# A written-out instruction order for attention plus a gated MLP on one core: no-ops between the halves of matmul pairs allowed on four queues, and a new order

## The chip, the core and the metric

The kernel runs on one core of a Trainium2 chip. The metric is the device time of one execution in microseconds. Three runs of the kernel before gave 153.65, 155.31 and 155.96 us; their median, 155.31 us, is the time before.

The core has five instruction queues that matter here: TensorE (PE in the profile), VectorE (DVE), ScalarE (ACT), GpSimd (POOL) and SyncE (SP). Each works through its own instructions strictly in order, and they wait for each other through semaphores. SP does no arithmetic; it issues transfers. POOL also issues transfers.

## What is computed

One row of 2048 tokens, 448 wide, bf16 inputs. Cut to what matters:

```python
xn = layernorm(x)                                    # (2048, 448)
q, k, v = split(xn @ wqkv)                           # 16 heads of 28
# each token attends to 8 keys: itself and 2, 4, .. 14 tokens back
attn = softmax(einsum(q, k[gathered]) * 28 ** -0.5)  # masked where the index is negative
s = (attn @ v[gathered]) @ wo                        # (2048, 448)
g = silu(gelu(xn @ w1 + b1) @ w2 + b2)               # 448 -> 1792 -> 448
return x + s * g
```

## The kernel before: tiles, stages and what sets the order

Tokens are kept even ones first, odd ones second, so that a dilated window of 8 becomes a contiguous one. They are cut into 16 row tiles of 128 tokens, four to a chunk of 512; the chunks are numbered 0 to 3. The attention works instead in nine blocks of up to 228 queries, each with two halves (p = 0 and 1).

For every row tile t: the statistics of its rows (L353, L357) and the reciprocal deviation (L374 and L375 on POOL, four tiles at a time from tile 8 on) give the normalised rows `xn` (L387). For tiles 0 to 3 TensorE transposes them (L402); from tile 4 on a transposing transfer issued by SP does (L300, `xnT<-xn`). The buffer of `xn` has four slots, so a fifth tile is normalised only when the transfer of an earlier one has landed. From `xnT` come the projections: q and k (L478), v (L501), and the first layer of the MLP (L551, 14 column tiles m of 128 per chunk). Projected q and k are copied from PSUM to row-major tiles by ACT (L249) or DVE (L251), and one transposing transfer per row tile on SP (L300, `qkT<-qk_tok` or `qk_pair`) brings them into `qkT`. Projected v goes to DRAM by POOL (L294, `v_rows<-v_tok`) and comes back shifted, per block (L294, `v<-v_rows`).

A block of attention is: copies of its keys (L662), scores (L677), exponentials on ACT (L683), a mask multiply on DVE or POOL (L693), the sum over values (L708), a reciprocal and a scaling on DVE (L719, L724), a store of the rows to DRAM (L731, by POOL or SP), and a transposing read of two row tiles at a time (L300, `xnT<-o_rows` or `oT<-o_rows`). The second layer of the MLP (L577, and L603 for the last four tiles) needs both halves of `w2`, that is both 784 KB transfers of L287 (tasks S260 and S262); its bias is added on DVE (L619). The output projection (L742, L757) and the gating (L765, L767, L773) end a tile.

**Pairs.** Inner dimensions such as 448 = 3 * 128 + 64 leave half of the 128 rows of TensorE empty, so most matmuls are run as pairs `pair(a, b)` (L425) of two jobs, each using 64 rows. The first half of a pair (f1, task P) runs job a on the upper rows and job b on the lower rows, into two PSUM banks; the second half (f3, task P) swaps them, and it accumulates into the same banks. Between the halves stands a no-op on another queue (f2, L437): it waits for the last matmuls of the first half, and the second half waits for it.

```python
def f2(k):
    held["told"] = (nc.gpsimd if k.on == "POOL" else nc.sync).nop()
    for i in held["last"]:
        behind(held["told"], i)
```

The no-op costs its queue nothing but its place: whatever stands ahead of it on that queue comes first, and whatever stands behind it waits until the first half has ended.

**Order.** All work is 1032 tasks, numbered as they are added (`_Plan.add`, L85). `ORDER` (L17 to L62) lists every task once, as a letter for the engine and the number: P TensorE, V DVE, A ACT, G POOL, S SP, D the landing of a transfer (no instruction). `emit` (L98) goes through it and issues the instructions, so the position of a task in its engine's queue, the PSUM banks and buffer slots that it takes (first freed, first used) and, where a task allows several engines, the engine are all set by that text. The text is fixed; the kernel holds no planner and no cost model.

Before, 49 of the 61 no-ops are on POOL and 12 on SP: chunks 0 and 1 allow POOL alone, the rest either (`HOPS`, L14).

The tasks that the text below names:

| task | what it is |
| --- | --- |
| S258, S256 | loads of x for row tiles 12 to 15 and 8 to 11, 448 KB each |
| S262, S260 | loads of the two halves of w2, 784 KB each |
| S161, S207, S214, S230, S237, S425 | transposing transfers of q and k of row tiles 3, 4, 5, 6, 7, 13 |
| S333, S337 | transposing transfers of xn of row tiles 10 and 11 |
| S929 | transposing read of attention rows of row tiles 4 and 5 |
| V229 / A229, P472 | copy of k of row tile 6 out of PSUM; first half of MLP layer 1, chunk 1, m = 0 and 1, which reuses its bank |
| P502, no-op 503, P504 | the pair of MLP layer 1, chunk 1, m = 12 and 13 |
| P209, no-op 210, P211 | the pair q, k of row tile 5 |
| P362, no-op 363, P364 | the pair q, k of row tile 10 |
| P436, no-op 437, P438 | the pair q, k of row tile 14 |
| P577 | first half of MLP layer 2 for row tiles 0 and 1 |
| V740, V589, P701 | first key copy of block 3; bias of row tile 2 of layer 2; value sum of block 1, p = 1 |
| P782 | value sum of block 4, p = 0 |
| G431, G460, G804, P812 | v of row tile 12 to DRAM; v of block 6 from DRAM; a mask of block 5; value sum of block 5, p = 0 |
| G278 | reciprocal deviation of row tiles 8 to 11 |

Of the kernel before, what the change touches and what calls it, by code (L numbers as in the profile page):

```python
# [18 lines left out]
G98 P5 S40 D41 S44 D45 P6 S46 D47 P7 G100 P8 V58 P9 V59 S74 D75 V62 A60 P10 S76 D77 P11 V61 V102 P12 P13 G649 V103 P14  # L19
V63 P104 A64 P105 G27 V106 A107 D108 S78 D79 G28 V65 P128 G31 V109 G29 V110 G30 P111 P112 V113 S80 D81 P132 A114 D115  # L20
P129 S84 D85 V66 P184 P133 V67 V70 A68 S86 D87 P130 V69 V116 P131 V117 V71 V185 P118 V101 A72 P119 V99 A52 V120 D121
S88 D89 P134 V73 V122 P149 V123 V136 A135 V146 P124 G150 P125 A139 P151 S137 D138 V126 D127 G147 D148 V142 P293 G140
D141 V152 P298 V153 G294 V94 S154 D155 P163 G299 V92 P295 V93 G164 V95 V90 G97 P300 A297 V143 P165 V82 A302 S144 D145
P313 V194 A166 V198 A296 V195 G167 D168 P308 V199 S196 D197 V83 V91 V169 G314 G96 A301 P315 S200 D201 P303 A316 G309
V186 G170 D171 V187 V190 A317 G172 D173 P310 V191 S188 D189 G304 G174 D175 P156 V650 A311 G176 D177 V651 P305 A312
# [6 lines left out]
P204 A501 P652 V205 P577 A500 S411 D412 V206 A53 G248 D249 V405 G250 D251 V406 S207 D208 A653 V401 P239 A655 G578 V402  # L32
G654 S407 D408 P579 G240 G656 S230 D231 S403 D404 P657 V583 P682 A658 P241 V580 A660 G659 P232 V245 A683 P362 V710
A685 G233 G661 V711 A584 P234 S363 V684 A242 P687 G920 G686 V236 P364 A235 V585 P586 A688 S237 D238 G243 D244 A690
V689 G246 D247 A581 G691 S921 D922 A366 V582 S923 D924 A365 P712 S367 D368 G587 P692 P662 V693 A713 P588 V663 V694
A715 V664 V695 V665 V696 V666 G697 D698 P346 V589 G667 D668 S669 D670 P717 V592 A590 G347 P671 G699 D700 P348 V672
A718 G252 D253 V673 P413 A349 G254 D255 V350 A720 P339 G414 V674 S351 D352 V675 A593 P415 G340 V740 G676 D677 P701
V714 A417 P341 G678 D679 V702 A416 V703 P595 A343 S418 D419 V716 V704 A342 V705 V741 G706 D707 S344 D345 V594 G708
D709 P722 V719 G596 P742 V723 P747 V724 A743 P597 S925 D926 A745 V725 V726 A748 V721 G727 D728 S729 D730 A750 V591
V744 V746 P731 V601 P376 V732 A602 V733 P369 G377 V734 P378 V735 G370 P353 V598 G738 S736 D737 D739 A382 S927 D928  # L40
V770 A599 P752 G383 D384 P371 V753 G354 V379 P355 A372 V754 G380 D381 P427 A356 V771 A359 P443 G357 D358 V755 V756
G360 D361 P772 V373 S444 S757 D758 P445 G428 G759 D760 A773 V749 S374 D375 P777 A775 V446 P429 A778 V751 P420 V800
A780 P761 V774 A447 G421 P422 V762 G385 D386 A430 V763 S448 D449 P450 G387 D388 A433 V764 V765 G389 D390 P604 A424
V423 G451 S766 D767 G391 D392 S929 D930 V776 G393 D394 V801 G395 D396 V603 G431 D432 S425 D426 V600 G434 D435 P452
V779 G605 P436 V781 G768 D769 A456 V453 P802 G457 D458 V830 S437 P438 A803 G454 D455 V831 P782 A805 P606 G804 V783
A440 V784 V785 V786 G460 D461 G462 D463 V439 S789 G787 D788 D790 V806 S441 D442 G459 P807 V610 P537 A808 V607 A810
P791 S538 P812 V809 A54 G464 D465 P512 V792 V793 G466 D467 P539 V794 S513 V795 A608 P514 V813 G798 S796 D797 D799 V814
A541 S931 D932 P527 V815 A540 V816 P532 G528 V811 A515 G817 D818 V609 G819 D820 P821 A611 P529 V860 G533 G468 D469
A516 V822 P534 V823 G470 D471 A531 P507 V824 V825 A536 V612 P522 G826 D827 S828 D829 A530 G508 A535 P509 S523 A861
P517 P952 S518 A511 P524 G953 A510 S933 D934 P954 A525 P519 V955 A526 P941 V959 G956 A521 V960 P832 P837 A520 G942  # L50
S957 D958 P943 S961 D962 A55 P613 V944 V948 V949 A838 S950 D951 A840 V839 V945 A833 P862 V841 S946 D947 G614 P867 A835
V834 P615 A868 V836 A870 G869 A863 A865 V864 G871 A890 P842 V619 P622 G866 V843 V844 A620 V845 A891 V846 V616 G847
D848 V621 P851 G849 D850 A617 S623 P892 P624 V852 A893 V853 A895 V854 V855 V618 G856 D857 V894 G858 D859 V896 P547
V628 V625 P963 A629 G548 A626 V630 P897 G964 P974 A898 V627 A900 P965 V899 G975 A56 V901 P542 S935 D936 V970 P976 V971
G543 V966 S972 D973 P549 V977 G967 P902 A551 P544 V903 V904 S968 D969 A550 P552 V905 V978 A546 V906 S979 D980 P872
G553 P554 A545 V981 S907 D908 P881 S909 D910 V873 A556 P572 V874 A555 V882 P567 V883 S573 V884 V885 P574 S568 V875
G886 D887 P569 V876 A575 G888 D889 V982 P996 A576 G877 D878 S983 D984 P557 A571 G997 G879 D880 A570 P998 S558 P911
V999 P559 V912 P562 V913 A560 V1000 A561 P985 V914 S563 S1001 D1002 V915 P564 S937 D938 V1003 G986 G918 P987 V1004
A565 P631 S1005 D1006 V992 A566 S916 D917 D919 V988 A57 V993 P632 V989 S994 D995 S990 D991 P635 V633 A634 S939 D940
P1012 P636 P1007 V637 P639 A638 V1008 V1009 V1013 S1010 D1011 P640 G1014 P643 S1015 D1016 V641 A642 P644 P1022 A645  # L60
P1017 V1023 V1024 P646 V1018 S1025 D1026 P647 P1027 V1019 A648 V1028 S1020 D1021 V1029 S1030 D1031
"""  # L62

# [59 lines left out]
def kernel(  # L123
# [12 lines left out]
    nc = tc.nc  # L136
# [8 lines left out]
    NMT = F // P  # L145
# [276 lines left out]
        tc.add_manual_dep(later.ins, earlier.ins.name,  # L422
                          mybir.DependencyInfo(mybir.DependencyClass.Sync, mybir.DependencyReason.DATA), reason="row tiles")

    def pair(a, b, early=False, n1=4, n2=3, after=(), give=()):  # L425
        held = {}

        def part(j, ps, kt, half, n):
            return lambda: j.part(ps, kt, half, n == 0, n == n1 + n2 - 1)

        def f1(k):
            p, q = buf(p_b, k, 0), buf(p_b, k, 1)
            held["last"] = together([part(a, p, kt, 0, kt) for kt in range(n1)], [part(b, q, kt, 1, kt) for kt in range(n1)])[-1]
        t = plan.add("PE", f1, a.deps + b.deps + a.late + b.late, take=(p_b, p_b) + a.into + b.into)

        def f2(k):
            held["told"] = (nc.gpsimd if k.on == "POOL" else nc.sync).nop()  # L437
# [124 lines left out]
    t_f2 = {}  # L562
# [6 lines left out]
    def ff2_pair(t):  # L569
        c, j = divmod(t, TPC)  # L570

        def job(t):
# [6 lines left out]
            def evac(a, own, i):  # L579
# [4 lines left out]
        t_f2[t] = pair(job(t), job(t + 1), False, NMT, NMT, [t_f2[t - 2]] if last else (),  # L584
                       tuple(h_at[(c, mt)] for mt in range(NMT)) if last else ())

    def ff2(t):
# [234 lines left out]
    def project(c):  # L822
# [3 lines left out]
        for i, t in enumerate((c * TPC, c * TPC + 2)):  # L826
            js = [[qk_rows(u, w) for w in range(2)] for u in (t, t + 1)]
            if not c and not i:
                first_batch([js[n] + [vs[n]] for n in range(2)], t)
            else:  # L830
                for n in range(2):
                    pair(*js[n], c < 2)
                pair(vs[2 * i], vs[2 * i + 1], c < 2)
# [33 lines left out]
    for c in range(NCH):  # L867
        hs = [ff1(c, mt) for mt in range(NMT)]
        for i in range(0, NMT, 2):
            pair(hs[i], hs[i + 1], c < 2)  # L870
        if c == 0:
            project(2)
            project(3)
# [59 lines left out]
```

## Time and profile before

| what | value |
| --- | --- |
| runs of the kernel before | 153.65, 155.31, 155.96 us |
| the profiled execution | 155.25 us, of which the span of the profile is 153.6 us |
| TensorE busy | 143.6 us of the span (94%) |
| DVE, ACT, POOL busy | 110.2, 88.5, 63.6 us |
| granted TensorE clock | 1.00 throughout |

The span runs from the first to the last instruction; 1.65 us of the execution lie outside it. Times in the views are microseconds from the start of the span. A group such as "PE bank L551 x8" is eight matmuls of line 551 in a row. In the timeline, the bracket at the end of a row is the idle time of the engine just before, and what ended it. L437 is a no-op between two halves; "SPq L437" is one on SP's queue.

### The profile page before, as it was taken

The numbers are of one execution on the slowest core, as the hardware profiler recorded it, in microseconds if no ns is written. First come the engines' busy times: TensorE is split into PE (matmuls) and PEld (weight loads), VectorE is DVE, ScalarE is ACT, GpSimd is POOL, SyncE is SP. The second block draws the span as 40 slices with busy tenths as digits, with TensorE's granted clock in tenths as the row PEclk, the third lists the DMA queues.
The fourth block names the chain that finished last, engine by engine and source line by source line (L and its number), as shares of the span: only waits on it lengthen the run. The fifth ranks groups of instructions, "written<-read, shape, count | busy, mean of one in ns | idle before, by whom it ended". The sixth has DMA issues, their size and how long they took to land.

```text
span 153.6 us, 4656 instructions
## 1 busy us (share of the span) xinstructions
PE 143.6 (94%) x1828; PEld 77.4 (50%) x1828; DVE 110.2 (72%) x295; ACT 88.5 (58%) x161; POOL 63.6 (41%) x119
## 2 busy tenths in 40 slices
PE   6999999977999959999999889999999999999991
PEld 2554555533455526556555446545555555445560
DVE  5689962068845795999999959925869999481542
ACT  3253576693485574374367227998895775672120
POOL 6833396002918490453274864742084022210200
PEclk9999999999999999999999999999999999999999
DMA  4999999999599898979689999981601242353301
GB/s 145 343 329 287 165 200 153 277 227 258 103 230 178 164 157 188 113 182 156 143 109 275 136 174 224 227 192 22 180 0 41 57 107 68 101 145 90 89 30 60
DMA packets 43950, 24.28 MB, mean 158 GB/s; under 512 B 33778, under 2 KB 41978, under 8 KB 43928
## 3 DMA queue, kind: packets, MB, share of 16 engines
q1 hardware_dynamic: 41080, 17.25, 58.7%
q0 software_dynamic: 2704, 6.62, 17.8%
q8 instruction: 14, 0.23, 0.7%
q10 hardware_dynamic: 144, 0.11, 0.2%
q14 instruction: 8, 0.07, 0.2%
HBM read 9.82 MB, written 6.29 MB: 105 GB/s over the span
## 4 chain that ended last, share of the span: by engine, by line
PE 64%; DMA 17%; DVE 11%; POOL 2%; issue 2%; SPq 1%; ACT 0%; POOLq 0%; DVEq 0%
PE bank L551 16%; PE bank L577 16%; PE bank L478 8%; PE bank L603 7%; DMA xnT<-xn 6%; PE bank L742 5%; DMA x_sb<-in_A_x_dram 5%; PE bank L501 4%; DMA v<-v_rows 4%; PE bank L264 3%; PE bank L708 3%; DVE kb L662 3%; DVE st L353 3%; DMA qkT<-qk_pair 2%; PE bank L677 2%
## 5 line engine op out<-in xcount | busy, mean ns | idle before, releaser
L551 PE MATMUL bank<-xnT,w 64*128 64x512 bf16 x392 | 47.3, 376 | 0.8 <-DVE qk_tok L251 0.8
L555 ACT ACTIVATE h<-bank,b 128x512 bf16<-128x512 f32 x56 | 35.2, 685 | 16.4 <-PE bank L551 16.0
L577 PE MATMUL bank<-w,h 64*128 64x448 bf16 x336 | 33.7, 349 | 0.0
L551 PEld LDWEIGHTS <-w 64*128 64x128 bf16 x392 | 20.3, 94 | 20.6 <-issue 1.8
L478 PE MATMUL bank<-w_in,xnT 64*128 64x448 bf16 (+1 forms) x212 | 26.8, 352 | 3.6 <-SPq L437 2.6
L683 ACT ACTIVATE E<-bank 128x456 bf16<-128x456 f32 (+1 forms) x36 | 17.4, 550 | 12.3 <-PE bank L677 10.2
L731 POOL DMA_DIRECT2D o_rows<-a x25 | 13.4, 540 | 25.1 <-DVE a L724 10.0
L577 PEld LDWEIGHTS <-h 64*128 64x128 bf16 x336 | 16.1, 94 | 13.9
L724 DVE TENSOR_TENSOR a<-bank,rd 114x448 bf16<-114x448 f32 (+1 forms) x36 | 22.2, 622 | 1.1
L294 POOL DMA_DIRECT2D v<-v_rows x22 | 13.6, 627 | 10.6 <-DMA v_rows<-v_tok 6.0
L478 PEld LDWEIGHTS <-xnT 64*128 64x128 bf16 (+1 forms) x212 | 10.3, 94 | 12.7 <-SPq L437 2.8
L353 DVE BATCH_NORM_STATS2 st<-x_sb 128x6 f32<-128x448 bf16 x16 | 9.5, 612 | 8.2 <-DMA x_sb<-in_A_x_dram 8.2
L501 PE MATMUL bank<-w_in,xnT 64*128 64x448 bf16 (+1 forms) x106 | 14.1, 351 | 0.0
L619 DVE TENSOR_TENSOR y<-bank,b 128x448 f32<-128x448 f32 x15 | 9.0, 621 | 6.3 <-PE bank L603 4.8
L294 POOL DMA_DIRECT2D v_rows<-v_tok x16 | 9.2, 576 | 7.4 <-DVE v_tok L251 4.6
L603 PE MATMUL bank<-w,h 128*128 128x448 bf16 (+2 forms) x70 | 11.4, 315 | 0.0
L693 POOL TENSOR_TENSOR E<-E,m_gen 128x456 bf16<-128x456 bf16 x8 | 8.5, 1076 | 6.4 <-ACT E L683 6.4
L631 ACT ACTIVATE t<-y 128x448 f32<-128x448 f32 x12 | 6.9, 579 | 7.2 <-DVE y L619 7.2
L662 DVE TENSOR_SCALAR kb<-qkT,plane 128x512 bf16<-128x512 bf16 x30 | 10.7, 410 | 0.2 <-DMA qkT<-qk_pair 0.2
L773 POOL TENSOR_TENSOR o<-x_sb,sg 128x448 bf16<-128x448 bf16 x3 | 3.1, 1030 | 17.8 <-DVE sg L767 9.1
L387 DVE TENSOR_SCALAR xn<-x_sb,mv,rstd 128x448 bf16<-128x448 bf16 x16 | 6.2, 396 | 5.8 <-DMA xnT<-xn 3.5
L693 DVE TENSOR_TENSOR E<-E,m_gen 128x456 bf16<-128x456 bf16 (+1 forms) x24 | 9.1, 391 | 1.4 <-ACT E L683 1.4
(80 smaller groups left out, 178.7 us busy)
## 6 DMA issues: line engine op xcount, KB each, us to landing
v_rows<-v_tok POOLq DMA_DIRECT2D x16, 128.0 KB, 4.0
v<-v_rows POOLq DMA_DIRECT2D x14, 128.0 KB, 4.3
out_dram<-o SPq DMA_DIRECT2D x15, 112.0 KB, 1.7
w<-in_B_w_dram SPq DMA_DIRECT2D x2, 784.0 KB, 14.4
o_rows<-a POOLq DMA_DIRECT2D x23, 64.1 KB, 2.7
w<-in_B_w_dram SPq DMA_DIRECT2D x2, 672.0 KB
x_sb<-in_A_x_dram SPq DMA_DIRECT2D x3, 448.0 KB, 6.2
w_in<-in_A_wqkv_dram SPq DMA_DIRECT2D x3, 336.0 KB, 3.9
```

What stands on the lines that cost most here:

```text
L294: nc.gpsimd.dma_start(dst(k), src())
L353: nc.vector.bn_stats(out=buf(p_st, k)[:], in_=x_sb[:, t, :])
L478: return nc.tensor.matmul(ps[:, :D], xnT[r, kt, cs], w, start=start, stop=stop)
L501: return nc.tensor.matmul(ps[:, :D], xnT[r, kt, k0:k0 + P], w, start=start, stop=stop)
L551: return nc.tensor.matmul(ps[:], w1[r, kt, ms], xnT[r, kt, cs], start=start, stop=stop)
L555: nc.scalar.activation(buf(p_h, own, i)[:], buf(p_b, own, i)[:], ACT.Gelu_apprx_tanh, bias=b1[:, mt:mt + 1])
L577: return nc.tensor.matmul(ps[:, :D], buf(*h_at[(c, mt)])[r, j * P:(j + 1) * P], w2[r, mt, :], start=start, stop=stop)
L603: nc.tensor.matmul(ps[:, :n], buf(*h_at[(c, mt)])[:, j * P:(j + 1) * P], w2[:, mt, cs], start=(mt == 0 and not biased), stop=(mt == NMT - 1))
L662: nc.vector.tensor_scalar(dst, src, plane[:, e:e + 1], None, op0=ALU.mult)
L683: nc.scalar.activation(buf(p_E, k)[:, :n], buf(p_b, a, r)[:, :n], ACT.Exp, scale=SCALE)
L693: (nc.gpsimd if k.on == "POOL" else nc.vector).tensor_tensor(out=E, in0=E, in1=m, op=ALU.mult)
L724: nc.vector.tensor_tensor(out=o, in0=sums(k, e)[:, :, :, :DH], in1=buf(p_rd, rd)[rows].unsqueeze(2).unsqueeze(3).to_broadcast((2 * nq, 8, ...
```

## The change

All functions but `pair` and its callers are as before. Three things change:

- A no-op may be on any of four queues, for every pair; the argument that kept chunks 0 and 1 on POOL is gone.
- The text of `ORDER` is new from its second line on. Of the 61 no-ops, 35 are now on POOL, 11 on SP, 9 on DVE and 6 on ACT.
- In that text, 46 tasks are on another engine than before: besides no-ops, seven copies of q or k go from DVE to ACT, two copies of v from ACT to DVE, eleven elementwise tasks (masks of L693, output sums of L773) from DVE to POOL and one back, and six stores of attention rows change between POOL and SP.

```diff
-HOPS = ("POOL", ("SP", "POOL"))
+HOPS = ("POOL", "SP", "ACT", "DVE")
...
-    def pair(a, b, early=False, n1=4, n2=3, after=(), give=()):
+    def pair(a, b, n1=4, n2=3, after=(), give=()):
...
-            held["told"] = (nc.gpsimd if k.on == "POOL" else nc.sync).nop()
+            held["told"] = {"POOL": nc.gpsimd, "SP": nc.sync, "ACT": nc.scalar, "DVE": nc.vector}[k.on].nop()
...
-        told = plan.add(HOPS[0] if early else HOPS[1], f2, [t])
+        told = plan.add(HOPS, f2, [t])
```

The part of `ORDER` around the loads, from the middle of chunk 0 to the first matmul of MLP layer 2 (P577):

```diff
-S192 D193 G157 G178 D179 P158 A307 P288 V159 A160 S258 D259 G264 D265 S256 D257 A306 P318 G289 S262 D263 G180 D181
-S260 D261 P290 G319 G182 D183 P225 A291 P320 A292 G226 P227 A322 P482 V281 A321 V283 S161 D162 P502 A228 G483 V284
-V229 P484 G503 V279 P492 A485 V270 V276 A486 P504 G493 V277 V280 P494 V272 A506 P472 V282 V273 A505 V274 V275 A495
-P209 V271 G473 V285 G278 A496 P474 V286 P216 G210 V331 G287 A475 V332 V335 S333 D334 P211 A476 V336 V327 P477 G217
-G268 D269 V213 S337 D338 G266 D267 V212 P218 V323 G478 P487 A219 V324 V328 S214 D215 A222 G220 D221 P479 G488 G223
-D224 V680 P489 A481 S329 D330 V681 P497 A490 V409 A480 P202 V410 S325 D326 G498 A491 V397 P499 G203 V398 S399 D400
-P204 A501 P652 V205 P577 ...
+V650 A312 G157 V651 P318 S258 D259 G264 D265 A307 G180 D181 A317 P158 G319 G182 D183 S256 D257 P288 A306 V159 A160
+P225 V289 P290 G226 P320 A291 P227 A322 S262 D263 P202 A321 P492 A228 G203 A292 P482 S161 D162 G493 A229 P204 V483
+V279 P484 A205 V281 P472 A206 V283 A485 P502 V280 V284 G473 V282 A486 V285 P474 V286 G287 P209 A475 V270 V276 P494
+A476 S503 S210 S260 D261 V272 P504 S207 D208 A495 V277 V273 P216 V271 V274 A506 P211 V275 A505 V409 G217 G278 V397
+P477 A496 V213 V398 A212 P218 G268 D269 V331 V332 A478 P497 V335 G266 D267 V219 S214 D215 P487 V222 G498 G220 D221
+V336 V680 G223 D224 P479 A488 S333 D334 V681 P489 A481 V410 P499 A490 S337 D338 P577 ...
```

On SP's queue this reads, before: S258, S256, S262, S260, S161, S333, S337, S214 and, four transfers of xn later, S207; after: S258, S256, S262, S161, no-op 503, no-op 210, S260, S207, S214, S333, S337. Further on, the no-op 363 goes from SP (behind S230 and the transfer of xn of row tile 13) to ACT, and the no-op 437, on SP in both, goes from behind S425 to ahead of it, still behind S929. V229 becomes A229.

More of the change, by code (lines that the diff above doesn't have):

```diff
@@ L32 @@
[L32 to L51, printed above, removed]
@@ new lines @@
+P477 A496 V213 V398 A212 P218 G268 D269 V331 V332 A478 P497 V335 G266 D267 V219 S214 D215 P487 V222 G498 G220 D221
+V336 V680 G223 D224 P479 A488 S333 D334 V681 P489 A481 V410 P499 A490 S337 D338 P577 A491 A480 S399 D400 A501 A500
+S411 D412 P652 V578 G248 D249 A53 P239 G250 D251 S230 D231 P579 V240 A653 A655 V654 V327 G656 V328 S329 D330 V323 P682
+V324 V583 P241 A683 V580 P232 S325 D326 A685 V684 A584 G686 P657 V245 P362 A658 V405 A660 V710 G233 P692 G659 P234
+A363 V693 A242 V694 P364 A235 G661 V695 P586 V696 A236 V711 A366 S237 D238 G243 D244 A581 V585 G246 D247 A365 V406
@@ new lines @@
+G697 D698 V401 S407 D408 V582 G699 D700 P712 V402 P662 G587 A713 P687 G920 S403 D404 V663 P588 V664 A715 G714 A688
+V716 V665 S367 D368 A690 V666 G691 V689 V740 S667 D668 P722 V589 P717 S669 D670 P346 A718 V723 V724 A720 P701 S921
+D922 G347 P348 V725 G252 D253 A590 V726 S923 D924 P413 G254 D255 A349 V702 S729 V703 G727 D728 D730 P339 V704 G414
+V705 P415 G340 V350 G706 D707 P671 A417 P341 V592 G708 D709 S351 D352 A416 P595 V741 A343 V672 V673 S418 D419 A342
+V674 A593 V675 V594 S344 D345 G676 D677 P742 V591 G678 D679 A596 P747 A743 P376 V719 A748 V721 S927 D928 P597 V744
@@ new lines @@
+G377 A750 G749 A745 G746 G751 S925 D926 P378 V601 P353 V598 A602 V379 P731 A382 G354 P355 V732 A599 G383 D384 V733
+P369 A356 G380 D381 V734 V735 P752 A359 G357 D358 P443 V370 V753 S736 D737 G360 D361 V754 P427 S738 D739 V755 S444
+V756 P445 G428 V770 G759 S757 D758 D760 P371 A447 V446 P761 A372 P429 V373 S448 D449 P420 G385 D386 V762 A430 V763
+G387 D388 A433 P450 V764 S374 D375 V771 G421 G389 D390 P422 V765 G451 G391 D392 P452 V800 S766 D767 A424 G393 D394
+S929 D930 V423 P436 G395 D396 A456 V453 G431 D432 P772 P777 V603 A773 P604 S437 G434 D435 S425 D426 V801 A778 G454
@@ new lines @@
+D455 V774 A780 G457 D458 V779 A775 V781 G768 D769 V600 V776 P438 S605 V830 G460 D461 P782 V439 A440 P802 G462 D463
+P606 A803 V783 S441 D442 G459 V784 A805 G804 V785 V786 V806 G787 D788 V831 G789 D790 P807 V607 P537 A808 V610 A810
+P791 S538 P812 V809 A54 G464 D465 P512 V792 V793 G466 D467 P539 V813 V794 S513 V814 A608 P514 V795 S931 D932 A541 P532
+V815 G798 V816 A540 P527 V811 S796 D797 D799 G533 G817 D818 A516 V609 G819 D820 P821 A515 V860 P534 G528 G468 D469
+V822 A611 V823 P529 G470 D471 A536 V824 P522 V825 A531 V612 G826 D827 S828 D829 P507 A530 S523 A535 P517 G508 A861
@@ L583, in ff2_pair @@
         last = j == TPC - 2
-        t_f2[t] = pair(job(t), job(t + 1), False, NMT, NMT, [t_f2[t - 2]] if last else (),
+        t_f2[t] = pair(job(t), job(t + 1), NMT, NMT, [t_f2[t - 2]] if last else (),
                        tuple(h_at[(c, mt)] for mt in range(NMT)) if last else ())
```

40 lines of the change are left out of this document (21 added, 19 removed).

## The prediction

> **What bounds the kernel now.** I read the page first: shares of the engines, then the chain that ended last.
>
> ```profile
> span 153.6 us, 4656 instructions
> PE 143.6 (94%) x1828; PEld 77.4 (50%) x1828; DVE 110.2 (72%) x295; ACT 88.5 (58%) x161; POOL 63.6 (41%) x119
> PE 64%; DMA 17%; DVE 11%; POOL 2%; issue 2%; SPq 1%; ACT 0%; POOLq 0%; DVEq 0%
> ```
>
> TensorE is busy 143.6 of 153.6 us, and the change alters none of its instructions, so at most the 10 us of idle time can be won. The timeline of TensorE says where they lie.
>
> ```profile
> 1.51 4.13 PE L264 MATMUL bank<-h 128*128 128x512 bf16 x13 [1.51 <-DVE eps_t L256]
> 33.87 1.02 PE L551 MATMUL bank<-xnT,w 64*128 64x512 bf16 x7 [0.79 <-DVE qk_tok L251]
> 37.85 0.74 PE L478 MATMUL bank<-w_in,xnT 64*128 64x448 bf16 x6 [0.81 <-POOLq L437]
> 56.47 0.74 PE L478 MATMUL bank<-w_in,xnT 64*128 64x448 bf16 x6 [1.86 <-SPq L437]
> 88.59 0.74 PE L478 MATMUL bank<-w_in,xnT 64*128 64x448 bf16 x6 [0.72 <-SPq L437]
> 89.77 0.39 PE L708 MATMUL bank<-v,E 64*128 64x58 bf16 x15 [0.42 <-DMA v<-v_rows]
> 149.88 0.36 PE L757 MATMUL bank<-wo,oT 128*128 128x112 bf16 x4
> ```
>
> Five stalls between 33 and 90 us sum to 0.79 + 0.81 + 1.86 + 0.72 + 0.42 = 4.60 us. The rest is the start (1.5 us and some tenths after it) and the tail (149.88 + 0.36 to 153.6: 3.4 us), whose tasks stand in the new order as before. The chain of waits, in order of time, and SP's timeline say why the stalls are there.
>
> ```profile
> 24.26 7.65 DMA x_sb<-in_A_x_dram
> 33.30 0.51 DVE qk_tok L251
> 39.54 9.33 DMA xnT<-xn x2
> 49.85 3.39 DMA qkT<-qk_pair
> 56.41 0.02 SPq L437
> ```
>
> ```profile
> 24.26 1.17 SPq L287 DMA_DIRECT2D x_sb<-in_A_x_dram  x2
> 25.48 4.34 SPq L287 DMA_DIRECT2D w<-in_B_w_dram  x2
> 29.93 8.22 SPq L300 DMA_TRANSPOSE qkT<-qk_pair  x1
> 52.54 2.51 SPq L300 DMA_TRANSPOSE qkT<-qk_tok  x1
> 55.14 1.22 SPq L300 DMA_TRANSPOSE xnT<-xn  x1
> 86.26 2.22 SPq L300 DMA_TRANSPOSE qkT<-qk_pair  x1
> ```
>
> Issuing S161 alone held SP for 8.22 us, from 29.93 to 38.15, behind 2.4 MB of bulk loads; an undisturbed issue takes 1.22. The queue of an engine that does no arithmetic thus reaches TensorE wherever a no-op stands on it.
>
> **The change part by part.** A no-op by itself is free: 17 ns. Its place is what counts.
>
> ```profile
> L437 SPq EVENT_SEMAPHORE x12: 17/17/17, 56.4 to 134.3; - x12
> ```
>
> Stall 1, 0.79 us: P472 waits for a PSUM bank that V229 frees, and V229 stood on DVE behind statistics that waited for S258 (the 7.65 us). As A229 on ACT it has no load ahead of it: -0.79. Stall 2, 0.81: no-op 210 stood on POOL behind G278, which waited for the statistics too. Now it is on SP: -0.81, if SP is free (below). Stall 3, 1.86: no-op 363 stood on SP behind the 2.51 and 1.22 us issues; now it is on ACT behind exponentials whose scores end before P362 does: -1.86. Stall 4, 0.72: no-op 437 stood behind the 2.22 us issue of S425; it now stands ahead of it, with 3.1 us of matmuls between P436 and P438 where there were 0.2: -0.72. Stall 5, 0.42: P782 waited for v of block 4. The tiles of v before it are projected earlier (P355, second half of tiles 8 and 9, comes 15 places sooner), while P782 keeps its place: -0.42. The floor is 155.25 - 4.60 = 150.65 us, against the profiled execution's own 155.25, which lies 0.06 under the median 155.31.
>
> What the new order adds, in the order of time. The chain of waits gives the clean lengths of TensorE's groups, and a group of its timeline a fixed point:
>
> ```profile
> 28.17 4.91 PE L551 MATMUL bank<-xnT,w 64*128 64x512 bf16 x43
> 93.03 0.86 PE bank L551 x8
> 103.84 0.65 PE bank L551 x6
> 74.74 0.76 PE bank L478 x8
> 77.04 0.57 PE bank L478 x6
> 57.21 2.65 PE bank L577 x28
> 59.86 0.22 PE bank L677 x16
> ```
>
> Up to 28.17 both orders give TensorE the same work. From there the new one has P202 (0.76), P492, P482 (0.86 each), P204 (0.57), P484 (0.65), P472, P502 (0.86 each), P474 (0.65), P209 (0.76), P494 (0.65): P504 is due at 35.65, P502 ends at 33.6, P209 at 35.0. Then 0.65 + 0.76 + 0.57 + 0.86 + 0.57 + 0.86 + 0.86 + 3 * 0.65 = 7.08: P577 is due at 42.73.
>
> ```profile
> w<-in_B_w_dram SPq DMA_DIRECT2D x2, 784.0 KB, 14.4
> qkT<-qk_tok SPq DMA_TRANSPOSE x10, 4.4
> v_rows<-v_tok POOLq DMA_DIRECT2D x16, 128.0 KB, 4.0
> wo<-in_A_wo_dram POOLq DMA_DIRECT2D x1, 336.0 KB, 4.5
> ```
>
> (a) No-ops 503 and 210 now stand on SP behind S161. If S161 held SP to 38.15 again, P504 would wait 2.5 us. But one 784 KB load fewer is ahead of it, so I expect it through before 35: from 0 to 2.5, taken 0.3.
>
> (b) S260 is issued only after no-op 210, at some 35.1 instead of behind S262 at 26; queued behind it are S207, S214, S333, S337, which feed DVE. P577 needs both halves. Landing in the 14.4 us of the row (with 2.4 MB in flight together) it comes at 49.5, 6.8 after P577 is due; at the 4.5 us of the 336 KB row it would come at 39.6, in time. With only two transfers left ahead of it I take it nearer the latter (784 / 336 * 4.5 = 10.5, 45.6, is what a strict scaling gives, and most of that is latency): from 0 to 6.8, taken 0.5. That S262 now has S161 and not S260 beside it costs nothing.
>
> The next rows price what moves between engines.
>
> ```profile
> L251 DVE CAST qk_tok<-bank 128x448 bf16<-128x448 f32 x11 | 6.5, 614 | 0.2 <-PE bank L478 0.2
> L249 ACT CAST qk_tok<-bank 128x448 bf16<-128x448 f32 x9 | 4.6, 535 | 2.2 <-PE bank L478 2.1
> L619 DVE TENSOR_TENSOR y<-bank,b 128x448 f32<-128x448 f32 x15 | 9.0, 621 | 6.3 <-PE bank L603 4.8 <-PE bank L577 0.7 <-DMA v<-v_rows 0.6
> L662 DVE TENSOR_SCALAR kb<-qkT,plane 128x512 bf16<-128x512 bf16 x30 | 10.7, 410 | 0.2 <-DMA qkT<-qk_pair 0.2
> L693 POOL TENSOR_TENSOR E<-E,m_gen 128x456 bf16<-128x456 bf16 x8 | 8.5, 1076 | 6.4 <-ACT E L683 6.4
> 26.00:46.00 20.00, 18.40 (x190) 9.05 (x188) 11.07 (x34) 12.86 (x22) 5.91 (x10) 1.00 1.07 213
> 66.00:92.00 26.00, 24.86 (x412) 14.09 (x410) 23.64 (x65) 13.09 (x27) 13.97 (x24) 1.00 1.00 168
> ```
>
> (c) V740 now stands ahead of V589 on DVE, 34 places earlier. Adding the groups from 42.73 on, P701 is due at 60.1 and needs the bank that V589 frees, so V740's two copies (2 * 0.41) and V589 (0.62) must begin by 58.6. They need S237, which cannot be issued before the second half of q, k of tile 7 (52.3) and its two copies on ACT: 53.7, landing 4.4 later, 58.1. Half a microsecond of margin on a transfer whose neighbours took 3.39 and 9.33 / 2: from 0 to 1.9 (the longest stall of that kind above), taken 0.4.
>
> (d) Thinner margins. Seven copies on ACT (7 * 0.54 = 3.8 us; ACT is busy 12.86 of 20 us there, so they are covered, and if not, each costs its 0.54) and eleven elementwise tasks on POOL, the masks at 1.08 each. DVE, 23.64 of 26 us busy from 66 to 92, gains. But G804 now stands on POOL behind G460, which waits for G431's landing (4.0), and P812 waits for G804; I get 0 to 0.7 there, and 0.1 to 0.3 each where P692 waits for a mask on POOL and P413 for a bank from DVE. From below: none, as 4.6 us of margin appear elsewhere; from above 3. Taken 0.9.
>
> Sum: 150.65 + 0.3 + 0.5 + 0.4 + 0.9 = 152.75, so **152.8 us**, 1.6% under the median.
>
> The stalls at hops on SP (1.86 and 0.72) hang on SP's issue time. [...]
>
> **The rivals.** First, the late half of w2, slower than before. Place: P577, behind S260. For it speaks the 14.4 us row and that the load starts 9 us later than before; against it that the queue ahead is shorter. At 14.4 us: 150.65 + 6.8 + 1.6 (the other three) = 159.0. It decides once S260 lands 3.0 us after P577 is due, at 45.7 or later: then the change is no gain; from about 48.9 on it is slower by over 2%, and S207 to S337 behind it, late too, add to that.
>
> Second, none of (a) to (d) shows: the margins are real, and the time is the floor, 150.65 to 151.4. For it: stretches without any idle time in the timeline before (90 to 149) show that such an order can run without gaps.
>
> Third, the hops wait elsewhere: ACT and DVE are busy engines, and a no-op on them waits for its turn as it did on SP. Then the 4.6 us come back in other places: 155.3. Against it: of 61 no-ops only three stopped a matmul before, all behind transfers or behind a wait for one.
>
> **How the numbers follow.** The forecast, 152.8 with 151.4 to 154.6 as its own range (each of the four taken sums from 0.75 to 4), has 0.42; the floor 0.20; the exchange 0.14; the late w2 0.24. A measurement of this kernel can tell about 2% from no change: faster is under 152.2, slower over 158.4. Faster: 0.20 and the lowest part of the forecast, 0.12, give 0.32. Slower: 0.18 of the late w2. Same: 0.50. The range, 150.8 to 159.0, reaches from the floor to the late w2 at its row's 14.4 us and leaves out some 0.15.
>
> **What would show it.** In the profile after: no idle bracket at P472, P211, P364, P438 and P782; SP free before 35.6 with L437 right behind the issue of S161; the second w2 load issued near 35 and no bracket "DMA w" on the first L577. TensorE idle between 30 and 92 of about 2 us, in pieces under 0.7. I am wrong if one bracket over 2 us stands at the first L577 (late w2), at a 6-matmul L551 group near 36 (S161 holds SP), or at second halves whose no-op is on ACT or DVE; or if the start or the tail, taken as unchanged, moves.

## The result, and the profile after

The changed kernel takes 161.68 us (median of 4 runs, 160.26 to 164.82); the kernel before took 154.48 us on the same chip (4 runs, 153.34 to 155.96). The ratio is 1.045, 95% interval 1.036 to 1.053: slower, and above the predicted range, which ended at 159.0. Medians and spreads, here and below, take all runs; ratios and intervals take only the runs within 1.5% of the fastest of the same kernel, here without 164.82 us. The profiled execution is one of 160.7 us.

From the page of the changed kernel: the span, the busy times, the granted clock in 40 slices, and the shares of the chain that ended last.

```profile
span 159.0 us, 4672 instructions
PE 147.3 (93%) x1828; PEld 94.5 (59%) x1828; DVE 105.9 (67%) x280; ACT 90.6 (57%) x166; POOL 73.2 (46%) x127
PEclk9999999999999999999998579999999999999998
PE 68%; DVE 15%; DMA 8%; issue 4%; POOL 1%; ACT 1%; SPq 1%; DVEq 0%; POOLq 0%
```

TensorE issues the same 1828 matmuls and is busy 3.7 us longer than before. Its granted clock fell somewhere: the 22nd to 24th slice show 8, 5 and 7. Now TensorE's timeline, the rows that answer to those of before; brackets hold the idle time ahead of a group and what ended it.

```profile
42.14 2.83 PE L577 MATMUL bank<-w,h 64*128 64x448 bf16 x28
...
59.23 0.37 PE L708 MATMUL bank<-v,E 64*128 64x58 bf16 x14 [0.23 <-DVE E L693]
61.37 0.40 PE L708 MATMUL bank<-v,E 64*128 64x58 bf16 x16 [0.45 <-DVE y L619]
...
86.00 0.20 PE L677 MATMUL bank<-qkT,kb 64*128 64x56 bf16 x1 [4.10 <-DVE kb L662]
86.79 0.56 PE L677 MATMUL bank<-qkT,kb 64*128 64x56 bf16 x16 [0.59 <-DVE a L724]
87.85 0.53 PE L677 MATMUL bank<-qkT,kb 64*128 64x56 bf16 x15 [0.51 <-DVE qk_pair L251]
88.18 5.36 PE L577 MATMUL bank<-w,h 64*128 64x448 bf16 x28
...
155.40 0.36 PE L757 MATMUL bank<-wo,oT 128*128 128x112 bf16 x4
```

All five old stalls are gone (SP's rows for steps (a) and (b) follow below), and until 81.9 us the changed kernel is ahead, by some 2.7 us (three stalls -4.2, the start -0.8, short waits +2.3). In the kernel before, the first scores of block 4 waited for nothing:

```profile
79.53 0.37 PE L677 MATMUL bank<-qkT,kb 64*128 64x56 bf16 x16
```

In the changed one TensorE stands for 4.10 us at them (P772), for 0.59 and 0.51 more just behind it, and the 28 matmuls after that take 5.36 us where the same group took 2.83 at 42.14. The granted clock says why (columns: window, its length, busy time of PE, PEld, DVE, ACT and POOL with instruction counts, granted clock, DMA share, GB/s):

```profile
76.00:82.00 6.00, 5.90 (x77) 2.91 (x72) 3.18 (x9) 3.19 (x6) 3.46 (x7) 1.00 0.83 161
82.00:88.00 6.00, 0.90 (x25) 0.67 (x27) 2.42 (x7) 0.54 (x1) 1.95 (x4) 0.86 0.86 158
88.00:94.00 6.00, 6.00 (x57) 4.76 (x53) 3.68 (x11) 1.42 (x3) 2.94 (x5) 0.57 0.94 195
```

TensorE worked 0.90 of the 6 us from 82 on. If the low clock is one half, which windows inside that stretch show (0.50), it lasted (0.14 + 0.43) * 6 * 2 = 6.8 us. What TensorE waited for is on DVE's timeline, the row with the largest bracket; SP's row shows what was issued meanwhile:

```profile
76.65 0.61 DVE L662 TENSOR_SCALAR kb<-qkT,plane 128x512 bf16<-128x512 bf16 x2
...
79.06 0.20 DVE L719 RECIPROCAL rd<-bank 114x8 f32<-114x8 f32 x1
85.58 0.62 DVE L662 TENSOR_SCALAR kb<-qkT,plane 128x512 bf16<-128x512 bf16 x2 [6.33 <-DMA qkT<-qk_tok]
```

```profile
77.90 3.54 SPq L300 DMA_TRANSPOSE qkT<-qk_tok  x2
```

The first key copy of block 4 (V770) runs at 76.65; the second (V771) reads the same columns, of tiles 7 and 8, and yet waits 6.33 us for a transposing transfer into qkT. In the new order S448 and S374, the transfers of tiles 15 and 11, are issued between the two: the two of SP's row. The compiled program lists what each instruction waits for; SP's 86 transfers take eight semaphores in turn (DMAHW0 to 7), S448 and S374 are on 5 and 6, and each of the two waits for the last one there:

```
SP  52 L300 DmaTransposeAnt qkT<-qk_tok_151 128x8x128 [waits DMAHW5_49,DVE_49,Activation_49]
SP  53 L300 DmaTransposeAnt qkT<-qk_tok_153 128x8x128 [waits DMAHW6_49,DVE_49,Activation_49]
DVE 160 L662 TensorScalarPtr kb_148<-qkT,plane 128x2x4x64 [waits DMAHW6_49,DMAHW5_49]
```

V771 waits for just these two. Its operand is a view with strides written by hand (`strided`, L520) that takes two key strips in each of four groups. Between its first and its last column lie those of tiles 11 and 15 as well, and the program orders it behind their writes although it reads none of them.

With both traces lined up group by group (from the start of a TensorE group to the start of the next), the last group's start moved by 155.40 - 149.88 = +5.5 us: start 0.8 shorter in this execution, in which the new order has no part; the five old stalls -5.6; P436 to P772 +4.3, the two scores +1.7, the 28 matmuls at half clock +2.45; the wait ahead of P701 +0.95; twelve short waits of 0.1 to 0.45 us +2.9; the rest -0.4. A bracket counts some tenths less than such a difference, since the ends of matmuls are modelled.

### The profile page after: what moved, and what is told of

Same layout as the page of the kernel before. It is cut to its first block, busy times and chain, and to the rows that moved or that the text cites. A ratio compares the mean times of both kernels' runs of the same rounds, so it can differ in the third digit from the quotient of the medians.

```text
span 159.0 us, 4672 instructions
## 1 busy us (share of the span) xinstructions
PE 147.3 (93%) x1828; PEld 94.5 (59%) x1828; DVE 105.9 (67%) x280; ACT 90.6 (57%) x166; POOL 73.2 (46%) x127
## 4 chain that ended last, share of the span: by engine, by line
PE 68%; DVE 15%; DMA 8%; issue 4%; POOL 1%; ACT 1%; SPq 1%; DVEq 0%; POOLq 0%
PE bank L551 26%; PE bank L577 15%; PE bank L478 7%; PE bank L603 6%; PE bank L742 4%; DMA x_sb<-in_A_x_dram 3%; PE bank L501 3%; DMA v<-v_rows 3%; DVE a L724 3%; DMA v_rows<-v_tok 2%; PE bank L708 2%; DVE y L619 2%; PE bank L677 2%; PE bank L757 1%; POOL v L294 1%
## 5 line engine op out<-in xcount | busy, mean ns | idle before, releaser
L551 PE MATMUL bank<-xnT,w 64*128 64x512 bf16 x392 | 48.7, 376 | 0.1
L577 PE MATMUL bank<-w,h 64*128 64x448 bf16 x336 | 36.7, 366 | 0.0
L551 PEld LDWEIGHTS <-w 64*128 64x128 bf16 x392 | 25.9, 94 | 15.2 <-issue 1.1
L577 PEld LDWEIGHTS <-h 64*128 64x128 bf16 x336 | 24.5, 98 | 8.5
L731 POOL DMA_DIRECT2D o_rows<-a x23 | 12.6, 551 | 16.9 <-DVE a L724 9.7
L693 POOL TENSOR_TENSOR E<-E,m_gen 128x456 bf16<-128x456 bf16 x15 | 16.1, 1093 | 8.6 <-ACT E L683 8.5
L478 PEld LDWEIGHTS <-xnT 64*128 64x128 bf16 (+1 forms) x212 | 11.4, 94 | 8.5 <-DVE xnT L251 0.6
L773 POOL TENSOR_TENSOR o<-x_sb,sg 128x448 bf16<-128x448 bf16 x7 | 7.2, 1031 | 11.7 <-DVE sg L767 8.6
L677 PE MATMUL bank<-qkT,kb 64*128 64x57 bf16 (+1 forms) x288 | 7.7, 190 | 5.3 <-DVE kb L662 4.1
L677 PEld LDWEIGHTS <-kb 64*128 64x128 bf16 x288 | 7.1, 96 | 7.1 <-DVE kb L662 5.1
```

Of the source, the lines that this page charges most:

```text
L478: return nc.tensor.matmul(ps[:, :D], xnT[r, kt, cs], w, start=start, stop=stop)
L551: return nc.tensor.matmul(ps[:], w1[r, kt, ms], xnT[r, kt, cs], start=start, stop=stop)
L577: return nc.tensor.matmul(ps[:, :D], buf(*h_at[(c, mt)])[r, j * P:(j + 1) * P], w2[r, mt, :], start=start, stop=stop)
L677: nc.tensor.matmul(buf(p_b, k, r)[:, c0:c0 + nq], buf(p_kb, t_kb[b][0])[h, 2 * p + i, g].rearrange("p e k -> p (e k)"), qkT[h, 0, g, q0:q0 ...
L693: (nc.gpsimd if k.on == "POOL" else nc.vector).tensor_tensor(out=E, in0=E, in1=m, op=ALU.mult)
L731: (nc.gpsimd if k.on == "POOL" else nc.sync).dma_start(o_rows[n + i * nq:n + i * nq + nq, :], buf(p_a, own)[i * nq:i * nq + nq, i, :])
```

## The experiments

Theory 1: a key copy waits for every transposing transfer of q, k that the program issues ahead of it, needed or not. Theory 2, the rival: its data or its engine are really late. A letter with its number in `ORDER` is called a word below. The first four kernels ran on one chip (the kernel before: 154.2 us median there).

**e1_keys_ahead**

```diff
-V770 G759 S757 D758 D760 P371 A447 V446 P761 A372 P429 V373 S448 D449
+V770 V771 G759 S757 D758 D760 P371 A447 V446 P761 A372 P429 V373 S448 D449
...
-S374 D375 V771 G421
+S374 D375 G421
```

> The changed kernel with one word of its order moved: V771, the second key copy of block 4, stands right behind the first (V770), ahead of S448 and S374, the transposing transfers of tiles 15 and 11. Theory 1 (the copy waits for every transposing transfer of q, k that the program issues ahead of it, needed or not): the wait of 6.33 us on DVE and TensorE's 4.10, 0.59 and 0.51 us at L677 go, TensorE isn't idle long enough for its clock to be halved, and 160.7 - 5.2 - 3.4 gives some 152 us. Theory 2 (the data of the copy, tiles 7 and 8, are really late, or DVE has no time for it): the stall stays within 1 us of where it is, 159 to 161 us.

158.78 us (157.3 to 159.35), ratio 1.034 (1.025 to 1.043). The stall of 4.10 went with the two behind it, so theory 1 named the right wait. But of the 8.7 us expected only some 3 came back, since two more waits show up behind it, on TensorE, and behind the second the clock is at half for another 3.4 us:

```profile
88.51 2.82 PE L576 MATMUL bank<-w,h 64*128 64x448 bf16 x28 [0.90 <-SPq L436]
...
95.24 0.50 PE L707 MATMUL bank<-v,E 64*128 64x58 bf16 x16 [2.60 <-POOL E L692]
```

(lines are one lower, as the order is written in one row fewer). The second is P812, which waits for the mask G804; e1's chain of waits follows it back:

```profile
84.52 7.79 DMA v_rows<-v_tok
...
92.86 0.54 POOL v L293
93.40 0.09 issue
93.48 0.62 POOL v L293
94.11 0.02 issue
94.12 1.07 POOL E L692
```

The write of v of tile 12 takes 7.79 us to land, the two loads of v of block 6 (G460, G462) wait for it on POOL, and G804 stands behind them. In the changed kernel this stall was hidden by the first one.

**e2_keys_between**

```diff
-A433 P450 V764 S374 D375 V771 G421
+A433 P450 V764 V771 S374 D375 G421
```

> The changed kernel with V771 moved to between S448 and S374, so that only the transfer of tile 15 is issued ahead of it. Theory 1: the copy begins when that transfer has landed (issued at 77.9, 4.4 us later 82.3), TensorE stalls 0.3 to 1.5 us at L677 instead of 4.10, and the time is 152 to 154 us. Theory 2: as the changed kernel, 159 to 161 us.

159.55 us (157.57 to 163.2), ratio 1.029 (1.018 to 1.041). The wait of V771 now ends with the landing of tile 15 alone, and the stall has the size that theory 1 gave it, 1.22 instead of 4.10 us. The time missed its 152 to 154. In the profiled execution, one of 160.85 us, P812 hardly waits; 0.60 and 0.68 us stand behind the 1.22, the clock is at half for 3.4 us after them, and there are 1.22 us at 30.0 (for a transfer of xn) and, new, 2.93 us at 55.7, taken up below.

```profile
86.24 0.20 PE L676 MATMUL bank<-qkT,kb 64*128 64x56 bf16 x1 [1.22 <-DVE kb L661]
```

**e3_exact_views**

```diff
+                for j in range(4 * (b == 4 and e)):
+                    k0 = strips[j][1]
+                    nc.vector.tensor_scalar(buf(p_kb, first)[:, j, :, e, :], qkT[:, 1, :, k0:k0 + NK], plane[:, e:e + 1], None,
+                                            op0=ALU.mult)
-                for j in range(2):
+                for j in range(0 if b == 4 and e else 2):
```

> The changed kernel, its order untouched; the second key copy of block 4 is written as four copies of one key strip each (plain slices of qkT, 128x256) instead of two that read two strips with a stride. The same numbers are computed. Theory 1 in its narrower form (it is the strided view, whose extent covers the columns of tiles 11 and 15, that makes the wait): no wait, stall gone, 152 to 153 us with some 0.4 us more work on DVE. If plain slices are held to wait as well, or the data are late (theory 2): 159 to 161 us.

160.17 us (157.81 to 165.36), ratio 1.032 (1.021 to 1.044). The median lies in the range expected if theory 1 were wrong, so the time alone doesn't decide, although the two lowest runs, 157.81 and 158.78, lie below all of the changed kernel's; the trace does. The order is that of the changed kernel, the data are the same, and the stall at P772 is gone. The four copies run while the two transfers, issued from 79.31 on, are still under way:

```profile
80.58 0.83 DVE L657 TENSOR_SCALAR kb<-qkT,plane 128x256 bf16<-128x256 bf16 x4
```

In the compiled program they wait for no transfer. So it was the way the view is written and not its data. Each of the four copies still reaches over the four groups of qkT, past columns of tiles 11 and 15, so a wide reach alone doesn't make the wait: here the copy through the hand-written view waited 6.33 us, and the four plain slices of the same data not at all. What is left is P812's 2.84 us, as in e1.

**e4_fed_pe**

```diff
         def f1(k):
+            for _ in range(18 * ((b, p) == (4, 0))):
+                nc.tensor.matmul(buf(p_b, k)[:], ident[:], w_in[:, 0, :512], start=True, stop=True)
             for g in range(G):
```

> The changed kernel, its order and its wait untouched; 18 matmuls of 512 columns, whose results the scores overwrite, stand ahead of the scores of block 4 and keep TensorE busy for some 4 us of the 4.10 us that it was idle. Theory A (the halved clock of 6.83 us comes from the idle time ahead of it): the granted clock stays 1.00 there, the 28 matmuls of L577 at 88 take 2.8 us and not 5.36, and the time is 160.7 - 2.5 to 3.4 = 157.3 to 158.2 us. Theory B (the clock falls there whatever TensorE does): 160 to 162 us.

161.08 us (159.23 to 163.96), ratio 1.041 (1.029 to 1.052); profiled execution 159.23, granted clock 1.00 throughout. The rows of its timeline that matter:

```profile
82.30 4.06 PE L673 MATMUL bank<-w_in,ident 128*128 128x512 bf16 x17
86.88 0.20 PE L679 MATMUL bank<-qkT,kb 64*128 64x56 bf16 x1 [0.52 <-DVE kb L662]
...
88.93 3.14 PE L577 MATMUL bank<-w,h 64*128 64x448 bf16 x28
```

The wait is the same, the 28 matmuls take 3.14 us instead of 5.36: 2.2 us of the loss were the clock, brought on by the idle time (theory A). The time alone would not say so: the profiled execution came out 1 us above the range of theory A, 0.89 of it a stall at 52 us that the changed kernel's profile hasn't, and the median lies in the range of theory B.

**e5_mask_first**

```diff
-G460 D461 P782 V439 A440 P802 G462 D463 P606 A803 V783 S441 D442 G459 V784 A805 G804
+P782 V439 A440 P802 P606 A803 V783 S441 D442 V784 A805 G804 G460 D461 G462 D463 G459
```

> The kernel of e1_keys_ahead (V771 behind V770), and besides the two loads of v of block 6 (G460, G462) and G459 behind the mask G804 on POOL, as they stood in the kernel before. Theory 3 (behind the first stall the changed order holds a second one: G804 stands on POOL behind G460, which waits 7.8 us for the write of v of tile 12): the 2.60 us at the values of block 4 (95.24 in e1's trace) go, and with them the clock loss behind them, 1.45 us in e1's trace: 158.8 - 2.8 - 1.45 = 154.5 us, 153.5 to 155.5. Rival (the exponential A803 or the mask itself is late): 2 us or more stay there, 157 to 159 us.

157.03 us (154.66 to 159.84), beside 154.16 for the kernel before on this chip; the runs lie too far apart for an interval of use (154.66 and 155.38 are in the range of theory 3, 158.69 and 159.84 are not). (The group at 95.24 that the expectation names is P812, of block 5, not 4.) The 2.60 us are gone, the profiled execution is one of 155.38 us at clock 1.00, and its largest bracket is the next in line, 1.83 us at P606 behind no-op 605, which stands on SP behind the issue of S425.

**e6_three_more**

```diff
-S605 V830
+A605 V830
...
-V740 S667 D668 P722 V589 P717
+S667 D668 P722 V589 V740 P717
```

> e5_mask_first with two more words: no-op 605 on ACT instead of SP, where it stood behind the issue of S425 (0.90 us at 88.51 in e1's trace), and V740, the first key copy of block 3, behind V589 instead of ahead of it (0.45 us idle, 0.95 us in all at the first half of q, k of tile 9). If both are what they seem: e5 less 0.9 and 0.95, 152.6 us, 151.7 to 153.7, and faster than the kernel before by 1 to 2%. If the order merely hands each stall to the next wait in line: the same as e5 within 1 us.

156.58 us (155.98 to 158.43), ratio 1.016 (1.008 to 1.025). A miss: both brackets are gone, but 0.94 us at 93.24 (behind a y on DVE), 0.40 at 81.42 (a no-op on POOL) and 0.34 at 63.12 took their place; between group starts the 0.95 from P346 to P701 is now 0.43 there and 0.52 at P348 behind it. The order hands its stalls on.

**e7_hops_alone**

```diff
-HOPS = ("POOL", ("SP", "POOL"))
+HOPS = ("POOL", "SP", "ACT", "DVE")
...
-V229
+A229
...
-G210
+A210
...
-S363
+A363
...
-S437
+A437
```

(the four words at their old places, and `pair` as in the changed kernel)

> The kernel before with its order kept, and only the other queues used: no-ops 210, 363 and 437 and the copy 229 on ACT, at their old places. If the stalls are a matter of the queue (as the prediction had it): 0.79, 0.81, 1.86 and 0.72 us go, 155.3 - 4.2 = 151.1 us in the profiled execution's terms, ratio to the kernel before 0.973. If a no-op on ACT waits for its turn as it did on SP (third rival of the prediction): 154 to 155 us, ratio 0.99 to 1.01.

152.14 us (151.93 to 152.2), ratio 0.989 (0.982 to 0.995): faster, by less than the 0.973 expected, and by its time as near the third rival's 0.99. The trace decides: none of the four stalls is left, and no no-op on ACT makes TensorE wait. One old wait grew, that of P782 for v of block 4, from 0.42 to 1.61 us, as everything ahead of it came earlier and the loads did not:

```profile
85.92 0.39 PE L707 MATMUL bank<-v,E 64*128 64x58 bf16 x15 [1.61 <-DMA v<-v_rows]
```

Between group starts the four stalls are worth -5.0 us, P782 +1.2 and four short waits, three of them at no-ops on POOL, +1.3; that leaves some 2.4 us. The rest of the 3.1 between the two profiled executions is a start that is 0.7 shorter in this one.

**e8_before_keys_behind**, the kernel before with the same false wait put in:

```diff
-V771 A359 P443 G357 D358 V755 V756 G360 D361 P772 V373 S444
+V373 S374 D375 V771 A359 P443 G357 D358 V755 V756 G360 D361 P772 S444
...
-V749 S374 D375 P777
+V749 P777
```

> The kernel before with one transposing transfer, tile 11 (S374, and the copy V373 that it needs), moved ahead of the second key copy of block 4 (V771), which needs only tiles 7 and 8. Theory 1 (a key copy waits for every transposing transfer issued ahead of it): V771 waits for the landing, 4.4 us after the issue at some 79, and TensorE stands at the scores of block 4 from 79.5 to 83 or 84, 3 to 5 us; 158 to 161 us. Theory 2 (the copy of block 4 is late in the changed kernel for another reason of its order): 154 to 156 us.

160.52 us (159.22 to 162.31), ratio 1.041 (1.030 to 1.051). One transfer that the block doesn't need, moved ahead of its copy, makes the old kernel nearly as slow as the changed one, stall and clock included:

```profile
81.31 0.77 PE L676 MATMUL bank<-qkT,kb 64*128 64x56 bf16 x16 [4.05 <-DVE kb L661]
PEclk9999999999999999999965999999999999999999
```

Theory 2 is out.

**e9_first_half** and **e10_second_half** join the two orders at P364; words that were done by then are left out of the second part, and twelve that the old order has ahead of P364 and the changed one behind it (406, 401, 402 and others) come first in e9's second part. The seams, against e7's order:

```diff
 e9
-V684 A242 P687 G920 G686 V236 P364 A235 V585 P586 A688
+G659 P234 A363 V693 A242 V694 P364 V406 V401 V402 S407 D408 S403 D404 G661 V711 P687 G920 V236 A235
 e10
-V236 P364 A235 V585 P586 A688
+V236 P364 P692 V693 V694 A235 V695 P586 V696 A366
```

> Two orders joined: the changed order up to P364 (the second half of the last projections of tile 10, some 52 us), then the order of e7_hops_alone. If the loss of the changed order lies behind P364: the time of e7, 152.1 us, 151.4 to 152.8. If its first part loses as well, by the steps (a) and (b) of the prediction (S161 ahead of two no-ops, the late second half of w2): 153 to 155 us.

> The other way round: the order of e7_hops_alone up to P364, then the changed order. If the loss lies behind P364: as the changed kernel, 160 to 163 us, with 4 us at the first scores of block 4. If it comes from both parts: 155 to 159 us.

e9: 157.52 us (156.25 to 158.9), ratio 1.028 (1.009 to 1.047). e10: 164.51 us (160.42 to 165.16) beside 154.61 for the kernel before on this chip. e10 has the stall at P772 (3.53 us) as expected, and its time lies above the 160 to 163 expected: its trace has 1.23 us at 38.5, 0.96 and 0.54 at 55 to 57 and a second stretch of half clock besides. e9 missed: the first part loses as well, though not by steps (a) or (b). Rows of e9's TensorE, DVE and POOL:

```profile
53.91 0.57 PE L707 MATMUL bank<-v,E 64*128 64x58 bf16 x16 [2.91 <-DVE v_tok L250]
```

```profile
49.57 3.75 DVE L692 TENSOR_TENSOR E<-E,m_gen 128x456 bf16<-128x456 bf16 x1
53.24 0.61 DVE L250 CAST v_tok<-bank 128x448 bf16<-128x448 f32 x1
```

```profile
50.01 3.05 POOL L692 TENSOR_TENSOR E<-E,m_gen 128x456 bf16<-128x456 bf16 x3
53.00 0.62 POOL L293 DMA_DIRECT2D v_rows<-v_tok  x1
```

DVE's mask V684, 0.39 us of work, takes 3.75 and ends 0.3 us after POOL's three masks do. e2 shows the same (3.77 us, and its 2.93 at 55.7). The changed order runs V684 just when these three run; the old one ran it at 55.9, behind them.

**e11_pv_later**

```diff
-P782 A805 P606 G804
+A805 P606 P782 G804
```

> e7_hops_alone with one word moved: P782, the values of block 4, behind P606 (28 matmuls, 2.65 us) instead of ahead of it, since in e7's trace it stands 1.61 us waiting for v of block 4. If that wait is all: 152.1 - 1.4 = 150.7 us, ratio to the kernel before 0.977. If the evacuations behind P782 hold something else up: 152 us as e7.

153.91 us (152.16 to 157.25), ratio 1.000 (0.993 to 1.007): a miss. P782's wait is gone, and three groups behind it wait 0.59, 0.29 and 0.46 us for DVE instead.

**e12_masks_back** (e6 with `G` turned to `V` in eleven words, 714 749 746 751 945 841 899 901 1000 1004 989) and **e13_trio_on_dve** (e9 with the same in 686, 659 and 661):

```diff
-G686 G659 G661
+V686 V659 V661
```

> e6_three_more with the eleven elementwise tasks that the change moved from DVE to POOL (masks 714, 749, 746, 751, 841, 899, 901 and the sums of the stores 945, 1000, 1004, 989) back on DVE, at their places in the changed order. Theory 4 (a DVE instruction that reads two tiles or copies bf16 from SBUF stands still while POOL works through elementwise instructions): the short waits of 0.2 to 0.45 us behind those tasks go, 156.6 - 1 to 2.5 = 154 to 155.6 us. If POOL's share is free, as step (d) had it, DVE only gets 11 * 0.4 us more work: 156.5 to 157.5 us.

> e9_first_half with the three masks 686, 659 and 661, which run one behind the other on POOL from 50 to 53 us, on DVE instead. In e9's trace DVE's own mask (V684) takes 3.75 us instead of 0.39, just as long as those three on POOL, and TensorE waits 2.91 us behind it. Theory 4: no DVE instruction there takes over 0.7 us, the 2.91 us go and with them the clock loss of 1.7 us: 157.5 - 2.9 - 1.0 to 1.7 + some tenths for 3 * 0.4 us more on DVE = 153 to 154 us. Rival (DVE stands still there for a reason of its own, as a late instruction load): the hole stays, 156 to 158 us.

e12: 156.86 us (154.91 to 159.24), ratio 1.013 (1.003 to 1.024), against 1.016 for e6: no gain that shows. The short waits ahead of 80 us and behind 119 us are where they were, so those are not POOL's doing. Between 80 and 94 us the trace did change: the 0.40 and 0.94 us of e6 are gone, and P782 waits 1.45 us for v of block 4 instead. e13: 156.93 us (156.41 to 158.15), ratio 1.026 (1.018 to 1.034). Its trace bears theory 4 out and its time does not:

```profile
49.61 0.91 DVE L692 TENSOR_TENSOR E<-E,m_gen 128x456 bf16<-128x456 bf16 x2
50.44 0.61 DVE L250 CAST v_tok<-bank 128x448 bf16<-128x448 f32 x1
...
53.79 1.40 DVE L661 TENSOR_SCALAR kb<-qkT,plane 128x512 bf16<-128x512 bf16 x2
```

```profile
55.78 4.49 PE L576 MATMUL bank<-w,h 64*128 64x448 bf16 x27 [2.41 <-DVE qk_tok L250]
```

With the three off POOL no mask on DVE is held up by more than some 0.2 us, and the wait behind V684 is gone. But DVE, which has no gap from 48.5 on, carries 1.2 us more, its key copy at 53.79, beside the one mask left on POOL, takes 1.40 us for 0.61 of work, and TensorE waits 2.41 us for a copy of q or k further on, with the same clock loss (0.987 to 0.989). Some of that load is the seam's, whose twelve words hold normalizations.

**e14_hops_again** is e7's kernel, unchanged, on another chip. (It, e12 and e13 share the runs of the kernel before: 154.43 us.)

> The kernel of e7_hops_alone once more, beside the two above and with more rounds, since e11, which differs from it by one word, came out at the time of the kernel before. If the no-ops' queues alone are worth what e7 showed: ratio 0.98 to 0.99. If e7's 0.9886 was luck of its runs: 0.995 to 1.005.

151.84 us (150.73 to 155.32), ratio 0.987 (0.979 to 0.996). It beats the kernel before by 1.3% (0.4 to 2.1%), and the changed one, by the two ratios (0.987 / 1.045), by some 5.5%.

## Why the prediction was wrong, step by step

- The five stalls: all gone from the changed kernel, 5.6 us between group starts, more than the 4.60 of the brackets. For four of them e7 shows that their queues were the cause. The fifth, P782's wait for a load, stands behind the new stall there and is settled less well: it is absent in e1, e5 and e6, and back with 1.61 us in e7 and 1.45 in e12, where the work ahead of it came earlier.
- (a), S161 ahead of two no-ops on SP, taken 0.3: right to be small. Its issue held SP for 4.49 us, not 8.22, to 30.53, and P504 (due 35.65) did not wait.
- (b), the late second half of w2, taken 0.5, and the first rival, 159.0: neither came. It was issued at 34.71, and P577 began at 42.14 (due 42.73) without a wait, so it had landed within 7.4 us of its issue, where the strict scaling of the 336 KB row gave 10.5. SP's rows:

```profile
26.04 4.49 SPq L300 DMA_TRANSPOSE qkT<-qk_pair  x1
34.71 0.38 SPq L287 DMA_DIRECT2D w<-in_B_w_dram  x1
```

  The time lay above that rival's for another reason.
- (c), V740 ahead of V589, taken 0.4: right in place (P701, behind y), 0.45 by its bracket and 0.95 between group starts. e6 shows that moving V740 back wins half of it, and loses as much one group later.
- (d), thinner margins, taken 0.9 with 0 to 0.7 for G804 behind G460: the place was right and the size wrong. P812 waits 2.60 to 2.84 us as soon as nothing earlier hides it, since v of tile 12 lands in 7.79 us (e1), not in the 4.0 of the row, which is a median over the whole kernel. The other short waits came to 2.9 us.
- The step that failed is none of these. The sum had no term for the waits that the program itself adds when words of the order pass each other: V771, two transfers further back, was taken as the same copy with the same needs. That term measured 4.10 us, with 0.59 and 0.51 behind it (6.0 us between group starts). The prediction followed a moved word's own needs and its queue, and not what the word was moved behind.
- The clock was taken as 1.00 throughout, and so a stall of over 4 us was priced at its own length. It cost 2.2 to 2.45 us more. Idle stretches of 4.10 us (the changed kernel) and 4.05 us (e8) were followed by 6.8 and some 7 us at half clock. Shorter ones can be followed by it too: 2.60 us in e1 and 2.41 in e13 each were, by 3.4 us, and so were 1.22, 0.60 and 0.68 us close together in e2; 2.84 us in e3 and the 2.93 of e2 were not. What tells them apart was not shown.
- So of the 8.0 us between the sum and the profiled execution (160.7 - 152.75), the missing term with its clock makes some 8.4; (c) and (d), 2.6 above what was taken for them, are about made up for by (a) and (b), by the larger stalls and by the shorter start.
- The second rival (the floor, 150.65) did not come. The old order with the new queues gets near it: medians of 152.14 and 151.84, and e14's lowest run is 150.73. The third (no-ops wait elsewhere) is refuted for ACT by e7; in the changed kernel's trace no idle bracket of TensorE ends with a no-op on ACT or DVE either.

What stays open: of the twelve short waits, nine (2.2 us) stay at the same groups in e1, e5, e6 and e12. Neither POOL's share (e12) nor V740's place (e6) makes them. What decides which instruction of DVE is held while POOL runs the three masks isn't settled either: in the changed kernel's profiled execution V684 ran in 0.55 us, and the key copies behind it were held instead (2.19 us for 0.61, until the masks ended), which cost TensorE some tenths at most.

## What to carry to other kernels

When an order is changed, list for each moved instruction what the compiled program makes it wait for, before and after. Here a view with hand-written strides was held behind writes to columns between its ends that it never read, so a transfer that slipped in between two such readers stopped the second; plain slices of the same data were not held. Look behind the first stall for the ones that it hides, and price a long stall of TensorE with a possible stretch at half clock after it: 3.4 us behind 2.41 in e13, 6.8 behind 4.10 in the changed kernel. Of a change in two parts, run each alone: here four words and their queues gave 1.3%, and the reordering around them lost some 6%.

## What the runs showed of the hardware

Some elementwise instructions on DVE took until POOL was through with its own: V684, 0.39 us of work, takes 3.75 us in e9, from 49.57 to 53.32, while three masks run on POOL from 50.01 to 53.06, and 3.77 in e2. Two key copies take 2.19 us for 0.61 in the changed kernel, from 51.19 to 53.38, with three masks on POOL from 49.92 to 53.23, and 1.40 for 0.61 beside one mask in e13, while a copy out of PSUM amid POOL's masks kept its 0.61 (at 50.15 in the changed kernel). e13, which takes the three masks off POOL, takes the hold of the mask away: two masks on DVE take 0.91 us there. What in the hardware holds DVE was not shown.

TensorE's granted clock in the changed kernel was 1.00 from 4.43 to 86.34, 0.50 to 93.17 and 1.00 again to 158.02. These stretches of 81.9, 6.8 and 64.8 us are 24, 2 and 19 times 3.41 us. In e8 the half clock lasted some 7 us (mean clock 0.978 over a span of 158.2); in e2, e9 and e13 it lasted 3.4 or 3.5 (0.989 over 159.2, 155.0 and 154.7), in e1 3.4 behind the 2.60 us, and in e10 two such stretches came to 6.8 (0.979 over 162.3). In the changed kernel TensorE was idle for 3.21 of the last 3.41 us at full clock and for 0.95 of the first 3.41 at half clock, behind which the half clock lasted another 3.41.

The size of a transfer alone didn't set its landing time here: the same write of 128 KB took 3.99 us at 76.3 and 7.79 at 84.5 in e1. What made the difference was not tested; the core's DMA engines were busier during the second (1.17 against 0.93 in the column of their share).

```profile
76.34 3.99 DMA v_rows<-v_tok
```
